# A fused attention and two-layer expert kernel: fewer and larger loads for attention, v on GpSimd's queue, and the stage's order planned anew

## The chip, the cores and the metric

The kernel runs on one core of a Trainium2 chip. The metric is the device time of one execution in microseconds (us), the median of several runs. One execution is also profiled, and the trace of that one is read here.

## The reference, cut to what matters

Three parts follow each other. Attention runs over 4 batches of 12 heads (448 positions, head size 64) with a soft cap. A dense part multiplies two projections and folds w3 and w_out behind them. A routed part sends every token through one of 8 experts.

```python
scores = cap * np.tanh((q @ k.T / sqrt(64)) / cap)
attn = softmax(scores) @ v                      # 4 x 12 heads, 448 x 64
x = attn as (1792, 768)
x = ((x @ w1) * (x @ w2)) @ w3 @ w_out          # w1, w2: 768 x 1024; w3: 1024 x 1024; float64 inputs
e = argmax(x @ w_gate + modality_bias[modality_id])
out = gate * (relu(x @ m1[e]) @ m2[e])          # 8 experts
```

The weights w1, w2, w3 and w_out are float64 in memory. The kernel turns them into float32 with integer operations on VectorE.

## The kernel before, in words

The change lies in the first stage, which holds attention and, beside it, work on the weights that attention does not depend on.

Attention goes by pairs of heads, 24 of them. For pair p the kernel loads k, q and v (`load_k`, `load_q`, `load_v`, lines 431 to 448), turns k and q with TensorE (`tr_k` L461, `tr_q` L475) and copies the results out of PSUM (`k_out`, `q_out`). The scores come in four blocks of keys c = 3, 0, 1, 2 (`score`, L488). ScalarE takes tanh (L493, L496 for the short block 3) and exp (L499) of each block. TensorE multiplies the blocks with v (`pv`, L508), the last block of one pair together with the first scores of the next (`pv_score`). VectorE adds the blocks for the softmax sums (`psum`, L524 to L528), TensorE spreads them (`sum_mm`, L535), and the results are stored (`sum_store` L544, `pair_store` L555).

Beside it stand three chains. Fourteen chunks of w_out, w1 and w2 are loaded (`load1`, tile raw, L289), made float32 (`narrow_a` L224 on ScalarE or L226 on VectorE, `narrow_b` L234 to L244), split into a rounded part wh (L252 or L254) and a rest wl (L329, on GpSimd). Sixteen chunks of w3 go the same way (`load_w3` L608, tile w3raw), are turned by TensorE (L620) and multiplied with w_out (`fold`, L649 to L651; 32 halves of 12 matmuls). The eight chunks of w_out are also multiplied with w_gate (`tr_wo` L585, `wo_gate` L593).

The order on every engine is not written by hand. A planner, class `Schedule`, takes each piece of work as a task with an engine (or several to choose from), a cost in ns, a key, and the tasks and buffers that it waits for. It repeatedly takes the task that can start earliest by its own costs, among equals the one with the smallest key, and writes its instructions at the end of its engine's queue. Keys count quarter pairs: pair p stands at 4p. So a changed cost or key moves instructions on all engines. On the chip each engine then works through its queue strictly in that order.

Buffers bound how far the stage runs ahead: two score tiles in PSUM (sc), two pairs of raw k and q, three v tiles, two raw weight chunks, two w3 chunks. A load of the chunk after next waits until the chunk in its buffer is used up. All loads and stores of the stage are issued from SyncE's queue (SP). TensorE keeps running dummy turns (L751) until the first k arrives.

After the stage come the dense part (L1001 to L1035) and the routed part (L1165 to L1216), which the change leaves as they are.

Of the kernel before, what the change touches and what calls it, by code (L numbers as in the profile page):

```python
# [120 lines left out]
def attention_moe_moe_kernel(  # L121
# [608 lines left out]
    def leave_at2():  # L730
# [32 lines left out]
    cap_in = add("SP", 475, -7 + 0.6, load_cap, dma=5)
    wg_in = add("SP", 475, -4, load_wg, dma=100)
    cap_in = add("DVE", 144, -100, inverse, [cap_in])


# [12 lines left out]
            wo_u[c] = ws.part  # L780
    for c in range(NW):
        u = c // 2
        key = (3 + 5.0 * c) if c < 8 else (10 + 10.0 * c)
        raw, y, un = ("wraw", c), ("y", c), ("unit", u)
        t = add("SP", 475, key - 2, ws.load1, take=[raw], use=[raw], dma=2185, deps=[ld])
        ld = t
        t = add({'ACT': (830, 0), 'DVE': (600, 300)}, 0, key, ws.abs1, [t] + ([ca] if c else []), take=[y], use=[raw, y])
        ca = t
        t = add({'DVE': (630, 0)}, 0, key, lambda eng: ws.narrow1(0, ENG[eng]), [t] + cn3[-1:], use=[raw, y])
        for i in range(1, 4):  # L790
            t = add("DVE", 630 if i == 1 else 950, key, do(narrow_c, c, i), [t], use=[raw, y])
        cn3.append(t)
        if c < 8:
            tt, tp = [("tr", "o", c, j) for j in range(2)], ("tr", "g", c)
            kg = key + 3.0
            cps = []
            for j in range(2):
                x = add("PE", 320, kg, do(tr_wo, c, j), [cn3[-1], *gate[-1:], *cps[-1:]], take=[tt[j], *([] if j else [("th", "o", c)])], use=[tt[j], y, ("th", "o", c)])
                cps.append(add({'ACT': (500, 0), 'DVE': (520, 300)}, 0, kg, lambda eng, c=c, j=j: wo_copy(c, j, eng), [x], use=[tt[j], ("th", "o", c)]))
# [22 lines left out]
    for p in range(NP + 1):  # L822
# [4 lines left out]
            dep, take, use = [ex[3], lv], [pk], [pk, ("th3", p - 1), ("v", p - 1)]  # L827
        if p < NP:
            k0, kk = 4 * p - 7, 4 * p - 4.0
            lk = add("SP", 1900, k0, do(load_k, p), take=[raw], use=[raw], dma=640)  # L830
            lq = add("SP", 950, k0 + 0.1, do(load_q, p), [(lk, 0)], use=[raw], dma=640)
            lv = add("SP", 1900, k0 + 4.0, do(load_v, p), [(lk, 0)], take=[vk], use=[vk], dma=640)
            t = add("PE", 380, 4 * p - 4.2, do(tr_k, p), [lk], take=[hk], use=[hk, raw])
            kl = add({'DVE': (620, 0), 'ACT': (530, 300)}, 0, kk, lambda eng, p=p: k_out(p, eng), [t], take=[kt], use=[hk, kt])
            t = add("PE", 380, 4 * p - 4.2, do(tr_q, p), [lq], take=[hq], use=[hq, raw])
            last_at2.append(t)
            ql = add({'DVE': (620, 0), 'ACT': (530, 300)}, 0, kk, lambda eng, p=p: q_out(p, eng), [t], take=[qt], use=[hq, qt])
            dep, take, use = dep + [kl, ql], take + [("sc", p, 3)], use + [("sc", p, 3), kt, qt]
        joint = add("PE", 770, 4 * p, do(pv_score, p), dep, take=take, use=use, mode="tiles")
        if p:  # L840

            for c in range(3):
                vl[p - 1, c] = add("PE", 770, 4 * p + c + 0.8, do(pv, p - 1, c), [ex[c], joint, vl.get((p - 1, c - 1))],
                                   use=[pk, ("th", p - 1, c), ("v", p - 1)], mode="tiles")
            smk = ("sc", "s", p - 1)
            sm = add("PE", 770, 4 * p + 2.9, do(sum_mm, p - 1), [ad], take=[smk], use=[smk, ("sums", p - 1)], mode="tiles")
            t = add({'ACT': (950, 0), 'DVE': (1000, 0)}, 0, 4 * p - 1, lambda eng, p=p: sum_out(p - 1, eng), [sm], take=[("smt", p - 1)], use=[smk, ("smt", p - 1)])
            ss = add("SP", 950, 4 * p, do(sum_store, p - 1), [t], use=[("smt", p - 1)], dma=25)
            t = add("ACT", 530, 4 * p - 2, do(pv_copy, p - 1), [vl[p - 1, 2]], take=[("pvs", p - 1)], use=[pk, ("pvs", p - 1)])
            po[p - 1] = add("DVE", 620, 4 * p - 2, do(pv_out, p - 1), [t], use=[pk, ("pvs", p - 1)])  # L850
            st[p - 1] = add("SP", 475, 4 * p, do(pair_store, p - 1), [po[p - 1]], use=[("pvs", p - 1)], dma=640)
            last_at1 += [sm, ss] if p > NP - 2 else []
            b, r = divmod(p - 1, H // 2)
            if r == H // 2 - 1 and b < B - 1:
                t = add("SP", 475, 4 * p, lambda b=b: rs_t.__setitem__(b, sums_in(b)), [ss], dma=100)
                t = add("DVE", 500, 4 * p, lambda b=b: sums_add(rs_t[b]), [t])
                last_at2.append(add("SP", 475, 4 * p, lambda b=b: sums_out(b, rs_t[b]), [t], dma=100))
        if p == NP:
            break
        ex, ad = {}, None  # L860
# [6 lines left out]
            t = add("ACT", 600 if c == 3 else 950, i + 0.2, do(p_tanh, p, c), [t, cap_in], take=[th], use=[sc, th])  # L867
            ex[c] = add("ACT", 580 if c == 3 else 950, i + 1.1, do(p_exp, p, c), [t], use=[th])
        for c in (1, 2, 3):
            ad = add("DVE", 620 if c == 3 else 1080, 4 * p, do(psum, p, c), [ex[c], *([ex[0]] if c == 1 else []), ad],  # L870
                     take=[sk] if c == 1 else [], use=[sk, ("th3", p) if c == 3 else ("th", p, c), *([("th", p, 0)] if c == 1 else [])])


# [17 lines left out]


    fs, wl_, fe = {}, {}, {}
    FK = lambda n, half: 4 * (4 + 0.62 * (2 * n + half)) + 2.3
    prev = None
    for n, (f, g) in enumerate(SWEEP):
        key = 12 + n * 5.5
        raw, r_, h_, w_ = ("w3raw", n), ("w3r", n), ("tr", "w", n), ("w3t", n)
        t = add("SP", 475, key - 3, do(load_w3, n), take=[raw], use=[raw], dma=1456)
        t = add({'ACT': (660, 0), 'DVE': (610, 300)}, 0, key, lambda eng, n=n: abs_w3(n, eng), [t], take=[r_], use=[raw, r_])  # L900
# [421 lines left out]
```

## Time and profile before

| what | us |
|---|---|
| median of three runs (986.35, 988.36, 1000.87) | 988.36 |
| the profiled execution | 979.18 |
| its span, first to last instruction | 977.5 |

The span stands for the kernel from its first to its last instruction; 1.68 us of the profiled execution lie around it. The first stage ends at about 323.5 us of the span, where the dense part's matmuls begin. In the rows an engine is PE (TensorE; PEld its weight loads), DVE (VectorE), ACT (ScalarE), POOL (GpSimd) or SP (SyncE). A q behind the name is the engine's sequencer, which issues DMAs. PEclk is TensorE's granted clock as a share of full speed. What stands behind "<-" is the event that ended an engine's idle time.

### The profile page before, as it was taken

Reading aid. Unit: us, or ns where it says so; the run is one execution under the profiler, and the core shown is the slowest. Engines: PE = TensorE matmul, PEld = TensorE weight load, DVE = VectorE, ACT = ScalarE, POOL = GpSimd, SP = SyncE. Lnnn points to the kernel's source line nnn. Section 1 sums busy time; section 2 is a strip of 40 time slices with the busy share of each in tenths; the row PEclk is TensorE's granted clock in tenths of the full one; section 3 lists DMA queues with packets and bytes.
Section 4 is the critical chain, followed back from the end, with each engine's and each line's share of the span. In section 5 each row is a group of like instructions: output and inputs, shape, how many; then the busy total and the mean of one; then the engine's idle time right before and its main releaser. Section 6 shows DMA issues by size and latency. Waiting matters only on the chain. (4 is left out here: it accounts for less than half of the span.)

```text
span 977.5 us, 13972 instructions
## 1 busy us (share of the span) xinstructions
PE 925.5 (95%) x5618; PEld 758.1 (78%) x5618; DVE 467.1 (48%) x668; ACT 377.0 (39%) x447; POOL 189.1 (19%) x114
## 2 busy tenths in 40 slices
PE   7789998999989899999999999999989999999994
PEld 4336665556544799999999999999879899889893
DVE  3678988695666477732005422110652533423410
ACT  4777777686857232222222211111421422322400
POOL 0111100020000112122542351300622311302011
PEclk9999999999999999999999999999999999999998
DMA  4755867665645556535633241301662491682411
GB/s 118 228 167 162 234 191 209 188 184 137 178 143 168 142 162 193 146 114 179 171 99 118 67 128 33 113 38 44 165 157 57 160 178 43 196 146 60 150 24 39
DMA packets 131736, 132.73 MB, mean 136 GB/s; under 512 B 61988, under 2 KB 114616, under 8 KB 131669
## 3 DMA queue, kind: packets, MB, share of 16 engines
q1 hardware_dynamic: 122388, 120.10, 42.9%
q0 software_dynamic: 9280, 11.71, 5.5%
q8 instruction: 46, 0.75, 0.3%
q14 instruction: 22, 0.17, 0.1%
HBM read 102.13 MB, written 30.19 MB: 135 GB/s over the span
## 5 line engine op out<-in xcount | busy, mean ns | idle before, releaser
L1002 PE MATMUL acc<-xT,wh 128*128 128x448 f32 x384 | 141.7, 369 | 0.7 <-DVE xT L936 0.7
L1001 PE MATMUL acc<-xT,wh 128*128 128x448 f32 x384 | 140.5, 366 | 1.9 <-ACT xT L934 1.9
L1003 PE MATMUL acc<-xT,wl 128*128 128x448 f32 x384 | 141.5, 368 | 0.0
L329 DVE TENSOR_TENSOR wl<-raw,wh 128x1536 fp32r<-128x1536 f32 (+1 forms) x42 | 73.5, 1758 | 121.3 <-ACT wh L252 121.3
L252 ACT CAST wh<-raw 128x1536 fp32r<-128x1536 f32 (+1 forms) x48 | 70.3, 1480 | 115.0 <-DMA raw<-in_moe_w_dram 82.6
L488 PE MATMUL sc<-QT,KT 64*64 64x448 f32 x672 | 93.2, 563 | 12.3 <-ACT th L493 5.9
L1208 PE MATMUL acc<-wl,hT 128*124 128x384 f32 x256 | 86.5, 338 | 3.7 <-DVE wl L329 3.7
L499 ACT ACTIVATE th<-th,capb 128x448 f32<-128x448 f32 (+1 forms) x96 | 89.3, 955 | 0.9
L508 PE MATMUL pv<-th,vt 64*64 64x448 f32 x672 | 89.0, 558 | 0.0
L1207 PE MATMUL acc<-wh,hT 128*124 128x384 f32 x256 | 87.6, 342 | 0.0
L1209 PE MATMUL acc<-wh,hT 128*124 128x384 f32 x256 | 86.5, 338 | 1.0 <-DVE hT L1186 1.0
L493 ACT ACTIVATE th<-sc,icap 128x896 f32<-128x896 f32 x72 | 71.5, 1007 | 23.5 <-PE sc L488 23.3
L1001 PEld LDWEIGHTS acc<-xT,wh 128*128 128x128 f32 x384 | 72.4, 189 | 9.2 <-ACT xT L934 2.6
L1002 PEld LDWEIGHTS acc<-xT,wh 128*128 128x128 f32 x384 | 72.6, 189 | 7.6 <-DVE xT L936 1.1
L1003 PEld LDWEIGHTS acc<-xT,wl 128*128 128x128 f32 x384 | 72.6, 189 | 5.5
L1033 PE MATMUL acc<-wh,gT 128*128 128x388 f32 x224 | 76.4, 341 | 0.0
L1034 PE MATMUL acc<-wl,gT 128*128 128x388 f32 x224 | 76.0, 339 | 0.0
L1035 PE MATMUL acc<-wh,gT 128*128 128x388 f32 x224 | 76.0, 339 | 0.0
L1181 PE MATMUL acc<-xsT,wh 128*128 128x496 f32 x192 | 74.7, 389 | 0.0
L1183 PE MATMUL acc<-xsT,wl 128*128 128x496 f32 x192 | 74.6, 389 | 0.0
L1182 PE MATMUL acc<-xsT,wh 128*128 128x496 f32 x192 | 74.4, 388 | 0.0
L1011 POOL TENSOR_TENSOR gT<-a,gT 128x896 fp32r<-128x896 f32 x16 | 43.8, 2739 | 145.7 <-DVE gT L1010 145.7
(159 smaller groups left out, 1543.2 us busy)
## 6 DMA issues: line engine op xcount, KB each, us to landing
raw<-in_moe_w_dram SPq DMA_DIRECT2D x48, 768.0 KB
w3raw<-in_moe_w_dram SPq DMA_DIRECT2D x16, 512.0 KB
raw<-w_scr SPq DMA_DIRECT2D x8, 776.0 KB
raw<-in_moe_w_out_dram SPq DMA_DIRECT2D x8, 768.0 KB
w_scr<-y SPq DMA_DIRECT2D x16, 384.0 KB
raw<-w_scr SPq DMA_DIRECT2D x8, 768.0 KB
q<-in_q_dram SPq DMA_DIRECT2D x48, 112.0 KB
x_scr<-pvs SPq DMA_DIRECT2D x24, 224.0 KB
```

Of the source, the lines that this page charges most:

```text
L488: mm(sc[rows_of(side(p, j, g)), g, :S], lhsT=KT[p][rows_of(j), o:o + D], rhs=QT[p][rows_of(j), :], start=True, stop=True)
L499: nc.scalar.activation(tht[p, c], tht[p, c], ACTF.Exp, scale=capb)
L508: mm(pvb[p][rows_of(j), r, :S], lhsT=vt[p][rows_of(r), NC * g + c, :], rhs=tht[p, c][rows_of(r), g, :] if c < NB else tht[p, c][rows_of(r) ...
L1001: mm(acc[:, ft, :S], lhsT=wh[:, o:o + P], rhs=x[:, 0, d, :], start=(d == 0), stop=False)
L1002: mm(acc[:, ft, :S], lhsT=wh[:, o:o + P], rhs=x[:, 1, d, :], start=False, stop=False)
L1003: mm(acc[:, ft, :S], lhsT=wl[:, o:o + P], rhs=x[:, 0, d, :], start=False, stop=(d == KD - 1))
L1033: mm(acc[:, hf, :HA], lhsT=gt[:, 0, f, ts], rhs=wh[:, o:o + HA], start=(f == 0), stop=False)
L1034: mm(acc[:, hf, :HA], lhsT=gt[:, 0, f, ts], rhs=wl[:, o:o + HA], start=False, stop=False)
L1035: mm(acc[:, hf, :HA], lhsT=gt[:, 1, f, ts], rhs=wh[:, o:o + HA], start=False, stop=(f == KF - 1))
L1207: mm(acc[:TP, hf, :HT], lhsT=ht[:, 0, f, cs], rhs=wh[:, o:o + HT], start=(f == 0), stop=False)
L1208: mm(acc[:TP, hf, :HT], lhsT=ht[:, 0, f, cs], rhs=wl[:, o:o + HT], start=False, stop=False)
L1209: mm(acc[:TP, hf, :HT], lhsT=ht[:, 1, f, cs], rhs=wh[:, o:o + HT], start=False, stop=(f == KF - 1))
```

## The change

In `load_k` the loads of the two heads are joined: one DMA for each half of the keys, so two in place of four for each pair. In `load_q` one DMA loads both heads in place of two, and that of pair 0 is issued from ScalarE's queue. The four DMAs of `load_v` are issued from GpSimd's queue. The bytes are the same, and so are the tiles that they land in.

The planner's numbers are changed to go with that, and others beside them: a DMA issue costs 630 instead of 475, the chunks of w_out get keys that lie 4.0 apart in place of 5.0, the turns of k and q are due a quarter pair earlier, the products with v 1.6 quarter pairs later, w3 and the folds are shifted, ScalarE is preferred less for the first step on w_out's chunks, and more for their copies.

```diff
         for g in range(2):
-            for j in range(2):
-                nc.sync.dma_start(k2[rows_of(g), 0:NC - g, j, :], keys(heads(k, p), g)[j])
+            nc.sync.dma_start(k2[rows_of(g), 0:NC - g], keys(heads(k, p), g).rearrange("h p c d -> p c h d"))
...
     def load_q(p):
-        for j in range(2):
-            nc.sync.dma_start(raw_qkv[p][1][:, :, j, :], heads(q, p)[j].rearrange("(p c) d -> p c d", c=NC))
+        eng = nc.sync if p else nc.scalar
+        eng.dma_start(raw_qkv[p][1], heads(q, p).rearrange("h (p c) d -> p c h d", c=NC))
...
             for j in range(2):
-                nc.sync.dma_start(vt[p][rows_of(side(p, j, g)), NC * g:NC + NB * g, :], keys(heads(v, p), g)[j])
+                nc.gpsimd.dma_start(vt[p][rows_of(side(p, j, g)), NC * g:NC + NB * g, :], keys(heads(v, p), g)[j])
...
-        key = (3 + 5.0 * c) if c < 8 else (10 + 10.0 * c)
+        key = (4.0 * c + 3) if c < 8 else (10 + 10.0 * c)
...
-            lv = add("SP", 1900, k0 + 4.0, do(load_v, p), [(lk, 0)], take=[vk], use=[vk], dma=640)
+            lv = add("POOL", 2800, k0 + 4.0, do(load_v, p), [(lk, 0)], take=[vk], use=[vk], dma=640)
```

Three places show how instructions move. The first is SyncE's queue from the first chunk of w_out (raw) to the second; k_180, q_181 and their like are the raw tiles of one pair, vt is v. Before:

```order
L289 DMA raw<-in_moe_w_out_dram 128x1536
L438 DMA k_180<-in_k_dram 64x4x64 x2
L438 DMA k_180<-in_k_dram 64x3x64 x2
L448 DMA vt<-in_v_dram 64x256 x2
L448 DMA vt<-in_v_dram 64x192 x2
L442 DMA q_181<-in_q_dram 112x4x64 x2
L438 DMA k_238<-in_k_dram 64x4x64 x2
L438 DMA k_238<-in_k_dram 64x3x64 x2
L448 DMA vt<-in_v_dram 64x256 x2
L448 DMA vt<-in_v_dram 64x192 x2
L442 DMA q_239<-in_q_dram 112x4x64 x2
L289 DMA raw<-in_moe_w_out_dram 128x1536
```

The same stretch of SyncE's queue after the change:

```order
L289 DMA raw<-in_moe_w_out_dram 128x1536
L607 DMA w3raw<-in_moe_w_dram 128x1024 x2
L437 DMA k_180<-in_k_dram 64x8x64
L437 DMA k_180<-in_k_dram 64x6x64
L441 DMA q_181<-in_q_dram 112x8x64
L437 DMA k_202<-in_k_dram 64x8x64
L437 DMA k_202<-in_k_dram 64x6x64
L441 DMA q_203<-in_q_dram 112x8x64
L289 DMA raw<-in_moe_w_out_dram 128x1536
```

Between the two chunks 20 DMAs stood, and now 8 stand, two of them the first w3 chunks, which stood behind the second w_out chunk before.

The second place is TensorE's queue from the start of the kernel: the dummy turns, the turns of k and q of pairs 0 and 1, the first scores (sc). Before:

```order
L751 MATMUL tr<-ident 128x128 x18
L461 MATMUL tr<-ident,k_99 128x128 x3
L461 MATMUL tr<-ident,k_99 128x64
L751 MATMUL tr<-ident 128x128 x12
L475 MATMUL tr<-ident,q_100 128x112 x4
L461 MATMUL tr<-ident,k_127 128x128 x3
L461 MATMUL tr<-ident,k_127 128x64
L488 MATMUL sc<-QT,KT 64x448 x10
L475 MATMUL tr<-ident,q_128 128x112 x4
L488 MATMUL sc<-QT,KT 64x448 x6
```

TensorE's queue from the start after the change:

```order
L750 MATMUL tr<-ident 128x128 x14
L460 MATMUL tr<-ident,k_99 128x128 x3
L460 MATMUL tr<-ident,k_99 128x64
L750 MATMUL tr<-ident 128x128 x16
L474 MATMUL tr<-ident,q_100 128x112 x4
L460 MATMUL tr<-ident,k_122 128x128 x3
L460 MATMUL tr<-ident,k_122 128x64
L474 MATMUL tr<-ident,q_123 128x112 x4
L487 MATMUL sc<-QT,KT 64x448 x16
```

The turn of pair 1's q now stands ahead of the first scores, where it stood between two groups of them.

The third place is GpSimd's queue at the last chunks of w1 and w2, where L329 makes the rest wl of one chunk. Before:

```order
L329 TENSOR_TENSOR wl<-y_1260,wh 128x6x128
L329 TENSOR_TENSOR wl<-y_1467,wh 128x6x128
L329 TENSOR_TENSOR wl<-y_1590,wh 128x6x128
L329 TENSOR_TENSOR wl<-y_1695,wh 128x6x128
L329 TENSOR_TENSOR wl<-y_1754,wh 128x6x128
L329 TENSOR_TENSOR wl<-y_2125,wh 128x6x128
```

GpSimd's queue at the last four of these chunks after the change:

```order
L329 TENSOR_TENSOR wl<-y_1303,wh 128x6x128
L447 DMA vt<-in_v_dram 64x256 x2
L447 DMA vt<-in_v_dram 64x192 x2
L329 TENSOR_TENSOR wl<-y_1392,wh 128x6x128
L329 TENSOR_TENSOR wl<-y_1569,wh 128x6x128
L329 TENSOR_TENSOR wl<-y_2110,wh 128x6x128
L447 DMA vt<-in_v_dram 64x256 x2
L447 DMA vt<-in_v_dram 64x192 x2
```

The loads of v now stand between the subtractions, so a load can be held up by a subtraction that waits for its chunk, and the other way round.

## Rows read from the trace of the kernel before

**Rows 1.** Windows: the stage's first 80 us, its rest, the parts behind it.
```profile
core 0: us, PE busy (x) PEld busy (x) DVE busy (x) ACT busy (x) POOL busy (x), PEclk, DMA share, GB/s
0.00:80.00 80.00, 62.59 (x491) 30.94 (x491) 50.66 (x82) 52.66 (x69) 7.89 (x10) 0.94 0.60 167
80.00:323.50 243.50, 230.80 (x1863) 138.87 (x1859) 183.65 (x287) 172.83 (x226) 21.39 (x21) 0.99 0.62 177
323.50:977.50 654.00, 632.13 (x3272) 588.27 (x3268) 232.79 (x301) 151.55 (x153) 159.78 (x83) 0.99 0.43 117
```

**Rows 2.** What ended TensorE's idle times from 0 to 82 us: total, times, longest.
```profile
PE sc L488 <- ACT th L493: 5.9, 3, 2.8
PE tr L475 <- DMA q<-in_q_dram: 4.1, 2, 2.2
PE tr L461 <- DMA k<-in_k_dram: 3.8, 3, 2.4
```

**Rows 3.** Timeline of SyncE's DMA issues, 0 to 14 us: start, duration, what.
```profile
0.86 2.63 SPq L438 DMA_DIRECT2D k<-in_k_dram  x4
3.54 1.30 SPq L442 DMA_DIRECT2D q<-in_q_dram  x2
...
6.01 2.51 SPq L438 DMA_DIRECT2D k<-in_k_dram  x4
...
11.13 1.26 SPq L442 DMA_DIRECT2D q<-in_q_dram  x2
```

**Rows 4.** Timeline of TensorE, 0 to 30 us: start, duration, idle before in brackets.
```profile
10.24 0.72 PE L461 MATMUL tr<-ident,k 128*128 128x128 f32 x4 [2.37 <-DMA k<-in_k_dram]
10.89 2.69 PE L488 MATMUL sc<-QT,KT 64*64 64x448 f32 x20
15.83 0.98 PE L475 MATMUL tr<-ident,q 112*128 112x112 f32 x4 [2.25 <-DMA q<-in_q_dram]
```

**Rows 5.** What ended ScalarE's idle times from 30 to 82 us.
```profile
ACT w3r L224 <- DMA w3raw<-in_moe_w_dram: 6.3, 2, 3.5
...
ACT y L224 <- DMA raw<-in_moe_w_out_dram: 2.4, 2, 1.5
```

**Rows 6.** Timeline of SyncE's DMA issues, 42 to 60 us.
```profile
43.79 2.77 SPq L448 DMA_DIRECT2D vt<-in_v_dram  x4
46.61 2.60 SPq L438 DMA_DIRECT2D k<-in_k_dram  x4
...
52.57 0.54 SPq L608 DMA_DIRECT2D w3raw<-in_moe_w_dram  x1
```

**Rows 7.** Timeline of ScalarE, 50 to 60 us.
```profile
56.88 0.66 ACT L224 ACTIVATE w3r<-w3raw 128x512 f32<-128x512 f32 x1 [3.45 <-DMA w3raw<-in_moe_w_dram]
57.45 0.99 ACT L493 ACTIVATE th<-sc,icap 128x896 f32<-128x896 f32 x1
```

**Rows 8.** Timeline of TensorE, 53 to 60 us.
```profile
58.49 0.98 PE L488 MATMUL sc<-QT,KT 64*64 64x448 f32 x8 [2.79 <-ACT th L493]
```

**Rows 9.** Windows of 20 us within the stage, columns as in the first group.
```profile
40.00:60.00 20.00, 14.36 (x117) 6.37 (x110) 13.60 (x25) 14.46 (x21) 2.16 (x2) 0.91 0.60 175
60.00:80.00 20.00, 19.12 (x158) 8.42 (x158) 19.37 (x28) 17.18 (x23) 3.40 (x2) 0.92 0.59 174
```

**Rows 10.** Timeline of ScalarE, 0 to 20 us.
```profile
8.31 1.28 ACT L496 ACT_TABLE_LOAD   x1 [8.31 <-DVE icap L759]
```

**Rows 11.** Groups of GpSimd's instructions, whole span: count, busy us, mean ns, idle before.
```profile
L1152 POOL DMA_INDIRECT xsr<-x_scr,idx x16 | 28.6, 1787 | 17.5 <-DMA idx<-tab_scr 10.9 <-issue 3.6 <-ACT a L1006 3.0
L329 POOL TENSOR_TENSOR wl<-y,wh 128x768 fp32r<-128x768 f32 x14 | 27.9, 1996 | 192.1 <-ACT wh L252 150.2 <-DVE wh L254 40.2 <-issue 1.8
...
L1149 POOL DMA_DIRECT2D idx<-tab_scr x4 | 2.4, 594 | 19.9 <-DMA out_dram<-y,idx 10.0 <-issue 9.9
```

**Rows 12.** Timeline of GpSimd, 55 to 64 us.
```profile
59.67 1.86 POOL L329 TENSOR_TENSOR wl<-y,wh 128x768 fp32r<-128x768 f32 x1 [15.00 <-ACT wh L252]
```

**Rows 13.** Timeline of VectorE, 57 to 64 us.
```profile
59.76 2.18 DVE L234 TENSOR_SCALAR y<-y 128x768 f32<-128x768 f32 x1
```

More of the change, by code (lines that the diff above doesn't have):

```diff
@@ L761, in inverse @@
         )
[L763 to L764 removed]
+    cap_in = add("SP", 630, -7 + 0.6, load_cap, dma=5)
+    wg_in = add("SP", 630, -4, load_wg, dma=100)
     cap_in = add("DVE", 144, -100, inverse, [cap_in])
@@ L782, in attention_moe_moe_kernel @@
         u = c // 2
-        key = (3 + 5.0 * c) if c < 8 else (10 + 10.0 * c)
+        key = (4.0 * c + 3) if c < 8 else (10 + 10.0 * c)
         raw, y, un = ("wraw", c), ("y", c), ("unit", u)
-        t = add("SP", 475, key - 2, ws.load1, take=[raw], use=[raw], dma=2185, deps=[ld])
+        t = add("SP", 630, key - 2, ws.load1, take=[raw], use=[raw], dma=2185, deps=[ld])
         ld = t
-        t = add({'ACT': (830, 0), 'DVE': (600, 300)}, 0, key, ws.abs1, [t] + ([ca] if c else []), take=[y], use=[raw, y])
+        t = add({'ACT': (920, 600), 'DVE': (600, 0)}, 0, key, ws.abs1, [t] + ([ca] if c else []), take=[y], use=[raw, y])
         ca = t
@@ L829, in attention_moe_moe_kernel @@
             k0, kk = 4 * p - 7, 4 * p - 4.0
-            lk = add("SP", 1900, k0, do(load_k, p), take=[raw], use=[raw], dma=640)
-            lq = add("SP", 950, k0 + 0.1, do(load_q, p), [(lk, 0)], use=[raw], dma=640)
-            lv = add("SP", 1900, k0 + 4.0, do(load_v, p), [(lk, 0)], take=[vk], use=[vk], dma=640)
-            t = add("PE", 380, 4 * p - 4.2, do(tr_k, p), [lk], take=[hk], use=[hk, raw])
+            lk = add("SP", 1260, k0, do(load_k, p), take=[raw], use=[raw], dma=640)
+            lq = add("SP" if p else "ACT", 630, k0 + 0.1, do(load_q, p), [(lk, 0)] if p else [], use=[raw], dma=640)
+            lv = add("POOL", 2800, k0 + 4.0, do(load_v, p), [(lk, 0)], take=[vk], use=[vk], dma=640)
+            t = add("PE", 380, 4 * p - 5.2, do(tr_k, p), [lk], take=[hk], use=[hk, raw])
             kl = add({'DVE': (620, 0), 'ACT': (530, 300)}, 0, kk, lambda eng, p=p: k_out(p, eng), [t], take=[kt], use=[hk, kt])
-            t = add("PE", 380, 4 * p - 4.2, do(tr_q, p), [lq], take=[hq], use=[hq, raw])
+            t = add("PE", 380, 4 * p - 5.2, do(tr_q, p), [lq], take=[hq], use=[hq, raw])
             last_at2.append(t)
@@ L869, in attention_moe_moe_kernel @@
         for c in (1, 2, 3):
-            ad = add("DVE", 620 if c == 3 else 1080, 4 * p, do(psum, p, c), [ex[c], *([ex[0]] if c == 1 else []), ad],
+            ad = add("DVE", 660 if c == 3 else 1120, 4 * p + 0, do(psum, p, c), [ex[c], *([ex[0]] if c == 1 else []), ad],
                      take=[sk] if c == 1 else [], use=[sk, ("th3", p) if c == 3 else ("th", p, c), *([("th", p, 0)] if c == 1 else [])])
@@ L893, in attention_moe_moe_kernel @@
     fs, wl_, fe = {}, {}, {}
-    FK = lambda n, half: 4 * (4 + 0.62 * (2 * n + half)) + 2.3
+    FK = lambda n, half: 18 + 2.48 * (2 * n + half) + 2.3
     prev = None
     for n, (f, g) in enumerate(SWEEP):
-        key = 12 + n * 5.5
+        key = 5.4 * (n + 2) + 3
         raw, r_, h_, w_ = ("w3raw", n), ("w3r", n), ("tr", "w", n), ("w3t", n)
-        t = add("SP", 475, key - 3, do(load_w3, n), take=[raw], use=[raw], dma=1456)
-        t = add({'ACT': (660, 0), 'DVE': (610, 300)}, 0, key, lambda eng, n=n: abs_w3(n, eng), [t], take=[r_], use=[raw, r_])
+        t = add("SP", 630, key - 3, do(load_w3, n), take=[raw], use=[raw], dma=1456)
+        t = add({'ACT': (660, -300), 'DVE': (610, 0)}, 0, key, lambda eng, n=n: abs_w3(n, eng), [t], take=[r_], use=[raw, r_])
         t = add({'DVE': (500, 0)}, 0, key, lambda eng, n=n: conv_w3(n, 0, eng), [t], use=[raw, r_])
@@ L906, in attention_moe_moe_kernel @@
         wl_[n] = t = add("DVE", 600, key - 4, do(w3_l, n), [t], use=[h_, w_])
-        lp = add("SP", 475 if g else 0, key - 3, do(part, n), [fs[n - KF]] if g else [], take=[("wst", n)], use=[("wst", n)],
+        lp = add("SP", 630 if g else 0, key - 3, do(part, n), [fs[n - KF]] if g else [], take=[("wst", n)], use=[("wst", n)],
                  lag=0, dma=1092 if g else None)
@@ L910, in attention_moe_moe_kernel @@
             fo = ("sc", "f", n)
-            late = vl[NP - 2, 2] if n == FN - 1 and half else None
+            late = vl[NP - 2, 2] if n == FN - 1 else None
             prev = add("PE", 2130, FK(n, half), do(fold, n, half), [t, units[2 * g], units[2 * g + 1], *augs[4 * g:4 * g + 4], prev, late],
@@ L914, in attention_moe_moe_kernel @@
             fe[n, half] = add("DVE", 560, 0, do(fold_out, n, half), [prev, lp], use=[fo, ("wst", n)])
-        fs[n] = add("SP", 475, key, do(fold_store, n), [fe[n, 0], fe[n, 1]], use=[("wst", n)], dma=1092)
+        fs[n] = add("SP", 630, key, do(fold_store, n), [fe[n, 0], fe[n, 1]], use=[("wst", n)], dma=1092)
     def leave_at1():
```

16 lines of the change are left out of this document (8 added, 8 removed).

## The prediction

> **What bounds the kernel now.** I read the windows first. The reader is to see in them that TensorE is busy nearly throughout, and that its free time is not spread evenly [rows 1]. Behind the first stage, from 323.5 us on, it works 632.13 of 654 us, and nothing there is touched. In the first stage it is idle for 80 − 62.59 = 17.4 us of the first 80 us, but only 243.5 − 230.8 = 12.7 us of the following 243.5 us. The granted clock adds to it: 0.94 of full speed over the first 80 us means 80 × 0.06 = 4.8 us of lost time, against 0.01 × 243.5 = 2.4 us later. So the first quarter of the stage loses 17.4 + 4.8 = 22.2 us and the other three quarters together 15.1 us. The place to look is the first 80 us.
>
> Second, the waits of TensorE in that stretch [rows 2]. Two kinds carry it: turns that wait for the DMAs of q and k (4.1 + 3.8 = 7.9 us) and scores that wait for ScalarE's tanh to free one of the two score tiles (5.9 us).
>
> Third, SyncE's own timeline. In the first 12 us it issues DMA after DMA without a pause, about 0.63 us each (2.51 us for 4) [rows 3]. Pair 1's k is fully issued at 8.52 us and TensorE gets it at 10.24; pair 1's q is issued by 12.39 us and used at 15.83 [rows 3, 4]. So a load lands 1.7 to 3.4 us behind its issue, and TensorE's 2.37 and 2.25 us of waiting are time that these loads stood in the queue. Around 50 us the same queue delays ScalarE. From 43.79 us SyncE is busy with v, with k and with what stands behind them, and the third w3 chunk is issued only at 52.57 [rows 6]. ScalarE, which works in order, waits 3.45 us for that chunk at a step that TensorE doesn't need soon, and the tanh behind it starts at 57.45 [rows 7]. TensorE's next scores wait 2.79 us for exactly that tanh [rows 8]. In this stretch ScalarE waits 6.3 + 2.4 = 8.7 us for raw weights [rows 5]. Both kinds of wait thus lead to one cause, SyncE's issue time, and after such gaps the granted clock is low: 0.91 and 0.92 from 40 to 80 us [rows 9].
>
> **The change part by part.**
>
> *Joined loads and v moved.* A pair costs SyncE 4 issues for k, 2 for q, 4 for v, 2 for sums and 1 for the result: 13 × 0.63 = 8.2 us, and a weight chunk or two on top. After the change it is 2 + 1 + 0 + 2 + 1 = 6, or 3.8 us. A joined load moves twice the bytes in runs of the same length. No row shows its issue; by the nearest row it takes 0.63 us, since the issue of a larger tile (a w3 chunk) takes 0.54 [rows 6]; that I take. The upper end is 1.3 (as two), at which k and q would save nothing and only v's 2.5 us a pair would be gone; the lower end, 0.54, saves half a microsecond more a pair. For the DMA engines the sum of bytes is unchanged; their share of 0.60 in the first 80 us would rise to about 0.70 if the same work fitted in 69 us, and the later window holds 0.62 with TensorE 95% busy [rows 1]. I cost that at nothing; if it is not hidden it appears as late weights.
>
> *Pair 0's q from ScalarE.* One issue of 0.63 us at a time when ScalarE has nothing to do (the first scores come at 10.89 [rows 4]). It costs nothing and takes 1.3 us of SyncE's queue from ahead of the cap and pair 1.
>
> *The head.* SyncE now issues k (2), cap, w_gate, k (2), q: 0.86 + 7 × 0.63 = 5.3 us. Pair 1's q lands 1.7 to 3.4 us later, at 7.0 to 8.7, and its turn stands ahead of the first scores. I put these at 8.4 us against 10.89, and the first tanh at 9.0. What is late next is ScalarE.
>
> *The first 80 us as a whole.* ScalarE does 52.66 us of work there, 1.3 of it a table load [rows 10] which the new order puts ahead of the first scores with a copy of k. The remaining 51.4 us must fit behind 9.0. In its densest 20 us ScalarE worked 17.18, or 86% [rows 9], in a window where loads were no longer late. At 86% the 51.4 us take 59.8, so the work of the first 80 us ends at 68.8: 11.2 us gained. Bounds: at 80%, 9.0 + 64.3 = 73.3 and 6.7 us gained; at 95%, 9.0 + 54.1 = 63.1 and 16.9 us gained. I take 86% because that row is the nearest. TensorE's own work there, 62.59 − 4.8 = 57.8 us, would fit as well. VectorE's 50.66 us fit behind 9.0 at its own densest 97% (19.37 of 20) by 61 us, so it isn't the last.
>
> *v on GpSimd's queue.* GpSimd gets 96 DMA issues. The nearest row is its plain DMA of 594 ns; its indirect one takes 1787 [rows 11]. So 57 us, at most 172 us, are added to 27.9 us of subtractions in a stage of 312 us. It is hidden in GpSimd's idle time at either end. A new wait arises where a load stands behind a subtraction that waits for its chunk. Behind it stand further loads and subtractions, and TensorE's product with v waits for the load. Three v tiles mean that a load can be issued once the pair three before is done, over a pair ahead of its use, some 13 us (323.5 / 24). I cost it at nothing, from −1 (v no longer queues behind weights) to +6 us. GpSimd can also hold up VectorE: a narrowing step took 2.18 us beside a subtraction of 1.86 that had begun just before [rows 12, 13]. If each of the some 24 v issues of the first 80 us did so for its 0.594, VectorE would have 14 us more, 50.66 + 14 = 65, ending at 9.0 + 65 / 0.97 = 76 us, and 4 us of gain would be left. That is the upper end. I take none, since the row shows it for a subtraction that reads and writes full tiles, which a DMA issue does not.
>
> The Trainium skill, SBUF — State Buffer, section "SBUF: two separate sides", warns of the other direction: while VectorE runs an operation in its two-port mode, GpSimd can't write the descriptors of its DMAs, and the section "A bandwidth-pool intuition that's wrong" gives such a DMA about 3.1 us in place of 0.62. By that figure, as an estimate, 96 issues would take 298 us and fill GpSimd, which is rival C below; no row of before shows a GpSimd DMA beside such an operation, though the rows on the subtraction agree that the two engines exclude each other.
>
> *The new order behind 80 us.* The same matmuls, the same tasks, other places. Idle 12.7 and clock 2.4 us could become anything from 9 to 21 us. I take no change, −6 to +6.
>
> Sum: −11.2 + 0 + 0. The profiled execution would take 979.18 − 11.2 = 968 us. Its median stands 9.2 us higher at 988.36, so the forecast for the median is 977 us.
>
> The Trainium skill, DMA: Bandwidth & Descriptors, section "Issuing engines are not separate DMA queues", says that issuing from several engines saves only the sequencer's time, usually small beside the DMA itself. The rows agree on what is saved and differ on its size: here that time was the last wait in most of 7.9 + 5.9 = 13.8 of the first 80 us. By the rule's "small" the sum would be near 0.
>
> **The rivals.**
>
> *A. The gain is larger.* ScalarE runs at 95% and the new order also saves the 6 us behind 80 us: 16.9 + 6 = 23, giving 965. For it: the late weights were 8.7 us of what ScalarE waited [rows 5]. Against: it has never been that dense over 20 us.
>
> *B. The gain is hidden.* VectorE, which turns w_out's chunks that now come faster, stays at the 68% of 40 to 60 us (13.60 of 20 [rows 9]): 9.0 + 50.66 / 0.68 = 83.5 us, no gain in the stretch; with the clock back, some 2 us: 986. For it: 19.37 of 20 in the next window shows that VectorE is nearly full once weights arrive. Against: that same density.
>
> *C. Slower: v's loads fill GpSimd.* If each issue takes so long that GpSimd's queue is the last, the stage lasts 27.9 + 96 × t. It decides from t = (312 − 27.9) / 96 = 2.96 us; at 3.3 us the stage takes 345 instead of 323.5, and the kernel 1010. Place: TensorE's products with v, which wait for their loads from the middle of the stage on. For it: that the two engines exclude each other [rows 12, 13]. Against: 0.594 and 1.787 are what such issues took, with VectorE in use too.
>
> **How the numbers follow.** Forecast 0.61 (its own range 971 to 984, from 16.9 us of gain to 4), A 0.17, B 0.17, C 0.05. Two per cent of 988.36 are 19.8 us, about what a measurement of this kernel can tell from no change; that is a bound at 968.6 and 1008. Faster holds nearly all of A: 0.17. Slower holds C and little else: 0.05. The rest is 0.78. The range takes in half of A and B whole: 964 to 989.
>
> **What would show it.** Right: TensorE's waits for q and k in the first 80 us fall from 7.9 to under 3 us, ScalarE's waits for raw weights from 8.7 to under 4 us, the first scores start near 8.4 us, the dense part begins near 312 us, and the windows behind 80 us lose about 15 us as before. Wrong: TensorE's waits keep their sum under other names (VectorE's sums, copies or narrowing), GpSimd's DMA issues take well over 1.8 us, or the dense part begins near 312 us but the end does not move.

## The result, and the profile after

The changed kernel takes 971.17 us (median of 4 runs, 968.68 to 977.17) against 987.36 for before (4 runs on the same chip, 979.43 to 1000.87). The ratio is 0.985, with a 95% interval of 0.981 to 0.990. That is 16.2 us between the medians, where 11.2 were forecast; 977 us was predicted in a range of 964 to 989. One of before's four runs, 1000.87, is a slow one; without it before's median is 986.35 and the difference 15.2 us.

The two profiled executions hide most of this. Their spans are 977.5 and 975.5 us, only 2.0 us apart. The profiled execution of after is the slowest of its four runs, at a mean granted clock of 0.975 (the other three had 0.983 to 0.987), and that of before, 979.18 us, is faster than all of its four, at 0.986. At one clock for both, 0.011 × 975.5 = 10.7 us more would lie between them, which brings the 2.0 to 12.7; this is an estimate, since it lets the whole span follow the clock. So the traces are read here for where the time went within them, and the medians for how much.

Windows of after: the first 80 us, the rest of the stage, what lies behind it (columns as in rows 1).

```profile
0.00:80.00 80.00, 70.81 (x512) 41.75 (x516) 58.02 (x91) 55.95 (x77) 28.09 (x40) 0.87 0.76 190
80.00:320.35 240.35, 226.58 (x1842) 136.74 (x1834) 178.89 (x279) 169.50 (x220) 52.46 (x87) 0.99 0.61 173
320.35:975.50 655.15, 634.19 (x3268) 590.86 (x3268) 231.97 (x300) 150.20 (x151) 159.77 (x83) 0.98 0.42 116
```

The first row answers to the first of [rows 1]. TensorE's idle time falls from 17.4 to 9.2 us, 8.2 won, and VectorE and ScalarE do 7.4 and 3.3 us more work in the same 80 us. The granted clock falls from 0.94 to 0.87: 10.4 us lost to it, where 4.8 were lost before. In this execution the clock takes back 5.6 of the 8.2 us. Behind 80 us TensorE stands idle for 13.8 us until the dense part, which begins at 320.35; in the trace of before it begins at 325.39 and that idle time is 14.6. So the stage is 5.0 us shorter (the forecast had its end near 312), and the 655.15 us behind it are 3.0 longer than before, at a clock of 0.98 instead of 0.99.

What ended TensorE's idle times in after, 0 to 82 us (total, times, longest), and then ScalarE's from 30 to 82 us:

```profile
PE tr L460 <- DMA k<-in_k_dram: 2.4, 2, 2.0
PE tr L592 <- DVE KT L254: 1.7, 1, 1.7
...
PE tr L619 <- DVE wl L598: 1.3, 1, 1.3
...
PE sc L487 <- ACT th L492: 0.6, 1, 0.6
...
PE tr L474 <- DMA q<-in_q_dram: 0.4, 1, 0.4
```

```profile
ACT woT L252 <- PE tr L584: 4.7, 3, 2.2
ACT smt L252 <- PE sc L534: 2.9, 2, 2.6
ACT th L492 <- PE sc L487: 2.2, 3, 1.1
ACT w3r L224 <- PE tr L619: 1.3, 1, 1.3
```

The waits for k and q were 7.9 us [rows 2] and are 2.8; the scores' wait for tanh was 5.9 and is 0.6. ScalarE's 8.7 us behind late raw weights [rows 5] are gone: TensorE and not a DMA is what it now waits for, 11.1 us by these four lines. Part of that is the new order and not the loads. It gives the first step on more of w_out's chunks to VectorE, and the kernel with the order only, below, shows the waits for raw weights there.

The head went another way than forecast. SyncE's DMA issues in after, 0 to 14 us, and TensorE's timeline, 0 to 16 us:

```profile
0.87 1.68 SPq L437 DMA_DIRECT2D k<-in_k_dram  x2
...
3.73 1.29 SPq L437 DMA_DIRECT2D k<-in_k_dram  x2
5.07 0.70 SPq L441 DMA_DIRECT2D q<-in_q_dram  x1
```

```profile
1.53 3.22 PE L750 MATMUL tr<-ident 128*128 128x128 f32 x14 [1.53 <-DVE ident L217]
6.77 0.72 PE L460 MATMUL tr<-ident,k 128*128 128x128 f32 x4 [2.02 <-DMA k<-in_k_dram]
7.42 3.16 PE L750 MATMUL tr<-ident 128*128 128x128 f32 x16
10.38 0.95 PE L474 MATMUL tr<-ident,q 112*128 112x112 f32 x4
...
12.58 2.69 PE L487 MATMUL sc<-QT,KT 64*64 64x448 f32 x20
```

Pair 1's q is issued by 5.77 us, near the forecast of 5.3. But k of pair 0, fully issued at 2.55, is turned only at 6.77, 4.2 us behind its issue. The 16 dummy turns behind it then take 3.16 us, behind the gap of 2.02. The granted clock of these microseconds, by windows:

```profile
7.00:9.00 2.00, 2.00 (x14) 1.76 (x13) 0.85 (x3) 0.00 (x0) 1.23 (x3) 0.75 1.25 200
9.00:11.00 2.00, 2.00 (x12) 2.00 (x11) 0.00 (x0) 0.00 (x0) 0.31 (x1) 0.50 1.17 256
```

It was 0.75 and then 0.50. The first scores come at 12.58, in before at 10.89 [rows 4].

### The profile page after: what moved, and what is told of

Read it like the earlier page. It is cut to its first block, busy times and chain, and to the rows that moved or that the text cites. A ratio compares the mean times of both kernels' runs of the same rounds, so it can differ in the third digit from the quotient of the medians.

```text
span 975.5 us, 13895 instructions
## 1 busy us (share of the span) xinstructions
PE 931.6 (95%) x5618; PEld 769.3 (79%) x5618; DVE 468.9 (48%) x668; ACT 375.6 (39%) x447; POOL 240.3 (25%) x210
## 5 line engine op out<-in xcount | busy, mean ns | idle before, releaser
L329 DVE TENSOR_TENSOR wl<-raw,wh 128x1536 fp32r<-128x1536 f32 (+1 forms) x42 | 73.5, 1758 | 113.3 <-ACT wh L252 113.3
L447 POOL DMA_DIRECT2D vt<-in_v_dram x96 | 50.7, 542 | 151.5 <-PE pv L507 149.9
L1180 PE MATMUL acc<-xsT,wh 128*128 128x496 f32 x192 | 74.7, 389 | 0.0
```

## The experiments

The theory that I took into them (theory 1): SyncE's issue time, 0.63 us for each DMA, is what the first quarter of the stage waits for, and the change wins by issuing less there. Its rivals: the new order of the engines wins it; the place of v wins it; or what a DMA moves, and how, counts and not its issue. Each group of runs was timed against before on its own chip, so before has a median for each group: 986.13, 986.95 and 985.97 us. Where two groups are compared below, that difference of up to 1 us comes on top of the noise.

**The parts apart.** Four kernels: the three load functions of the change in the old order; the new order with the old load functions; the change with v back on SyncE; the change with k and q in halves again.

```diff
 # loads only: before, with load_k, load_q, load_v of the change
 # order only: the change, with load_k, load_q, load_v of before
 # v on SyncE: the change, and in load_v
-                nc.gpsimd.dma_start(vt[p][...
+                nc.sync.dma_start(vt[p][...
 # k and q in halves: the change, and in load_k (load_q likewise, pair 0 on SyncE too)
-            nc.sync.dma_start(k2[rows_of(g), 0:NC - g], keys(heads(k, p), g).rearrange("h p c d -> p c h d"))
+            for j in range(2):
+                nc.sync.dma_start(k2[rows_of(g), 0:NC - g, j, :], keys(heads(k, p), g)[j])
```

> The kernel before with only the three load functions of the change: k in two DMAs and q in one for each pair, the first q from ScalarE's queue, v from GpSimd's. The planner still sees the old tasks, so TensorE, VectorE and ScalarE keep the order of the kernel before. Theory 1 (SyncE's issue time was what the first 80 us waited for): most of the gain is here, 8 to 13 us faster than before; TensorE's waits for k and q and ScalarE's waits for raw weights in the first 80 us fall from 7.9 and 8.7 us to under 4 each. Rival (the new order brings the gain): within 3 us of before, with the same waits under other names.

> The changed kernel with the three load functions of the kernel before: 4 + 2 + 4 DMAs for each pair, all from SyncE's queue, in the new order of tasks. Theory 1: the gain is gone or turned into a loss, 0 to 15 us slower than before, since the new order asks SyncE for weights earlier still; waits of TensorE for k and q of 8 us or more in the first 80 us. Rival (the order brings the gain): 8 us or more faster than before.

> The changed kernel with v's four DMAs for each pair issued from SyncE's queue again; k and q stay joined. SyncE then issues 10 DMAs for a pair in place of 6 (13 before). If issue time counts issue by issue, about half of the gain stays: 5 to 9 us faster than before. Rival (moving v off SyncE is what counts, since it waits there for TensorE to free a v tile and holds up the loads behind it): no more than 3 us of gain stay. Second rival (GpSimd's early v loads take the DMA engines from the first k and q): as fast as the change or faster, with the first scores ahead of 12.6 us.

> The changed kernel with k and q loaded by 4 + 2 DMAs from SyncE's queue again, the first q too; v stays on GpSimd's queue. SyncE issues 9 DMAs for a pair in place of 6. If issue time counts issue by issue, about half of the gain stays: 6 to 10 us faster than before, and the head of the kernel is later than in the change by some 2 us. If v on SyncE's queue was the whole of it: as fast as the change within 3 us.

| kernel | issues per pair on SyncE | us, median | ratio to before, 95% |
|---|---|---|---|
| before | 13 | 986.13 | |
| loads only, old order | 6 | 971.70 | 0.984 [0.980, 0.989] |
| order only | 13 | 985.95 | 1.000 [0.998, 1.003] |
| change, v on SyncE | 10 | 970.25 | 0.984 [0.980, 0.988] |
| change, k and q in halves | 9 | 979.56 | 0.994 [0.991, 0.997] |

The loads alone give the whole gain and the new order alone gives none: the order is out as a cause. With v back on SyncE nothing is lost, so v's loads standing in that queue are not what counted either. One sign that I had named failed: with the loads only, ScalarE still waits 6.3 us for raw weights (8.7 before, expected under 4), and the kernel gains 14.4 us all the same. But the last two rows are no straight line in the number of issues. Ten with k and q joined give all of it, nine with v moved and k and q in halves give 40%. So I asked next whether that is the issues at all.

**One load change at a time in the old order, and v held back.**

```diff
 # k and q joined, v on SyncE: before, with load_k and load_q of the change
 # v moved only: before, and in load_v
-                nc.sync.dma_start(vt[p][...
+                nc.gpsimd.dma_start(vt[p][...
 # v held: loads only, and in load_v ahead of the DMAs
+        if p < 3:
+            held = at1.tile([1, 1], F32, name="held", tag="held", bufs=1)
+            nc.gpsimd.tensor_copy(held, raw_qkv[p][1][0:1, 0, 0, 0:1])
```

> Before, with k by two DMAs and q by one; v stays on SyncE and the order of the other engines is the old one: 10 issues for a pair. Theory 1 (SyncE's issue time, any issue counts alike): 3 of 7 issues saved, so 40% of the gain, about 980 us. Theory 2 (what counts is how soon the last k and q of the first pairs have landed, so joining them is the whole of it): about 971 us, ratio 0.985, TensorE's waits for k and q in the first 82 us under 4 us.

> Before, with v issued by GpSimd and nothing else changed: 9 issues for a pair on SyncE. Theory 1: 4 of 7 issues saved, about 978 us. Theory 2: k and q still stand in 6 issues a pair, and v's loads now compete with them at the head: at most a third of the gain, 981 to 987 us, waits for k and q still over 4 us.

> The three load functions of the change in the old order (as in the run with the loads only), and GpSimd issues v of pairs 0 to 2 only once that pair's q has landed (a 1x1 copy on GpSimd reads q first). If v's early loads crowd the first k and q: the first k turn near 5.3 us instead of 6 to 7, the first scores some 1 us sooner, 968 to 971 us. If they don't: as the loads alone, 971.7 us within 2; if v is then late, TensorE waits for v tiles and it is slower than 973.

Measured against 986.95 for before: joined only 971.88, ratio 0.987 [0.984, 0.990]; v moved only 974.19, 0.990 [0.986, 0.994]; loads with v held 969.63, 0.986 [0.982, 0.989]. Either half of the change thus gives nearly everything by itself, and both together (971.70) no more than one. Both theories missed: theory 1 in its linear form expected 980 and 978, theory 2 expected at least 981 for v alone. In the old order it looks like a threshold. Added up from its timeline, SyncE's issuing takes 66.8 of the first 80 us before, 61.6 with k and q joined, 52.7 with v moved and 35.6 with both; the first step buys nearly everything. But that share alone doesn't decide: the change with k and q in halves issues for only 50.1 us and gains 6.6. What ends last beyond the first step? Windows from 20 to 60 us, of the loads only, of the loads with v held, and of k and q joined only:

```profile
20.00:60.00 40.00, 36.92 (x329) 18.51 (x322) 39.66 (x58) 38.08 (x53) 16.00 (x20) 1.00 0.80 209
```

```profile
20.00:60.00 40.00, 36.52 (x338) 17.56 (x333) 38.45 (x62) 36.93 (x51) 16.96 (x20) 1.00 0.89 228
```

```profile
20.00:60.00 40.00, 35.59 (x282) 16.36 (x278) 30.77 (x49) 32.60 (x45) 5.50 (x3) 0.87 0.71 197
```

In the first two VectorE works 39.66 and 38.45 of 40 us, ScalarE 38.08 and 36.93: they are full, and more could not be won there. With k and q joined only they are not, 30.77 and 32.60, and yet that kernel is as fast by its median. So why issues saved beyond the first step buy nothing is not shown.

Holding v back set the first k turn at 6.13 instead of 7.16 us and the first scores at 9.41 instead of 11.97 in the profiles, and is worth 2 us at most by the medians, within their uncertainty. The same edit was made in the changed kernel itself:

> The changed kernel, with v of pairs 0 to 2 issued by GpSimd only once that pair's q has landed (a 1x1 copy on GpSimd reads q first); the order of the other engines is the change's. If early v loads crowd the first k and q: the first k turn near 5.3 us instead of 6.77, the first scores near 11 us instead of 12.58, 966 to 970 us. If they don't: 971 us, the first scores near 12.6.

It took 972.66 us, 0.986 [0.981, 0.990]: no difference from the change. In its profile, the longest of its six runs (982.46), the first k turn came at 6.42 us instead of 6.77 and the first scores at 12.03 instead of 12.58. So v's early loads are a small part of the late head there (in the old order 1.0 us of the first k turn), and the 5.3 us that I expected for k was wrong.

**SyncE's issue time given back almost without bytes.** To the loads only (the old order) come seven blank DMAs for a pair, of 4 KB that nobody reads, so SyncE issues 13 again, while k, q and v travel as in the change.

```diff
+    def blank(p):
+        t = nc.dram_tensor(f"blank{len(blanks)}", (16, D), F32).ap()
+        blanks.append(t)
+        nc.sync.dma_start(t, q[0, 0, 0:16])      # or nc.gpsimd
...
             nc.sync.dma_start(k2[rows_of(g), 0:NC - g], ...)
+            blank(p)
...
         eng.dma_start(raw_qkv[p][1], ...)
+        blank(p)
...
+        for _ in range(4):
+            blank(p)
```

> The three load functions of the change in the old order, and on SyncE seven blank DMAs of 4 KB for a pair, between DRAM tensors that nobody reads, at the places where before had its other halves of k and q and its v: SyncE issues 13 for a pair again, but the bytes of k, q and v come as in the change. Theory 1 (issue time): the gain is gone, 984 to 988 us, and TensorE's waits for k and q are back at 6 us or more. Theory 2 in the form that the joined load itself lands sooner: most of the gain stays, 971 to 975 us.

> The run with seven blank DMAs for a pair, but GpSimd issues them: same 168 transfers of 4 KB, other sequencer. If it is SyncE's issue time that costs (theory 1): the 27 us of loss are gone, 970 to 976 us (a little of it may come back where GpSimd's subtractions or v get late). If the transfers themselves cost (write receipts, ring space, DMA engines): 990 us or more.

> Blank DMAs on SyncE for pairs 0 to 7 only, whose k is loaded in about the first 80 us: 56 of 168. If the cost of SyncE's issues sits in the first quarter of the stage, as the prediction has it: nearly the whole loss, 990 to 998 us. If it is spread evenly: a third of 27 us, 979 to 982 us.

> Blank DMAs on SyncE for pairs 8 to 23 only: 112 of 168. If the cost sits in the first quarter: 970 to 977 us. If it is spread evenly: two thirds of 27 us, 987 to 991 us.

| blank DMAs | us, median | ratio to before, 95% |
|---|---|---|
| 168 on SyncE, all pairs | 998.59 | 1.013 [1.009, 1.017] |
| 168 on GpSimd, all pairs | 971.82 | 0.986 [0.982, 0.991] |
| 56 on SyncE, pairs 0 to 7 | 987.32 | 1.002 [1.000, 1.005] |
| 112 on SyncE, pairs 8 to 23 | 976.47 | 0.992 [0.988, 0.995] |

The first row stands against 986.95 for before, the others against 985.97. The same 168 transfers cost 26.9 us from SyncE (998.59 − 971.70) and nothing measurable from GpSimd, so it is SyncE's queue and not the transfers. Nor do the blanks make a load in that queue land later: k is turned 3.8, 3.3 and 3.5 us behind its issue for pairs 0 to 2, and 4.6 for pair 0 with the loads only. That leaves the time of issuing. A third of the blanks, in the first pairs, takes back the whole gain (987.32 − 971.70 = 15.6 us; 0.28 us an issue). The other two thirds cost 4.8 us alone (0.04 an issue), about the uncertainty of the two medians, but 11.3 on top of the first third (998.59 − 987.32).

The place can be read more directly. TensorE's queue holds the same order in before and in these kernels, so one can ask when the 491 matmuls of before's first 80 us [rows 1] are done. Windows up to that moment, with the loads only, with the blanks in pairs 8 to 23, and with those in pairs 0 to 7:

```profile
0.00:67.40 67.40, 59.38 (x491) 31.43 (x491) 52.63 (x82) 50.96 (x69) 26.84 (x42) 1.00 0.83 200
0.00:68.30 68.30, 60.90 (x491) 31.29 (x491) 52.89 (x82) 51.29 (x69) 26.12 (x42) 0.95 0.80 197
0.00:85.00 85.00, 68.88 (x491) 34.36 (x491) 51.71 (x82) 52.84 (x70) 23.56 (x39) 0.86 0.60 160
```

The work of before's first 80 us takes 67.4 us with the loads only, 68.3 with blanks behind pair 7 and 85.0 with blanks up to pair 7; VectorE has done 82 instructions each time, as in before. Medians and traces agree: the gain is won in the first quarter of the stage, and issues of SyncE there take it back.

SyncE's queue, 5 to 20 us, then what ended TensorE's and ScalarE's idle times, 0 to 82 us, with all blanks on SyncE:

```profile
5.68 0.65 SPq L444 DMA_DIRECT2D k<-in_k_dram  x1
6.37 0.64 SPq L435 DMA_DIRECT2D blank<-in_q_dram  x1
...
7.74 3.16 SPq L435 DMA_DIRECT2D blank<-in_q_dram  x5
10.95 0.65 SPq L449 DMA_DIRECT2D q<-in_q_dram  x1
```

```profile
PE sc L498 <- ACT th L503: 7.6, 2, 7.2
PE tr L471 <- DMA k<-in_k_dram: 4.8, 4, 1.8
PE tr L485 <- DMA q<-in_q_dram: 1.9, 1, 1.9
```

```profile
ACT w3r L224 <- DMA w3raw<-in_moe_w_dram: 10.1, 2, 8.2
```

A blank DMA holds the queue for 0.63 us (3.16 for 5), as long as a joined k (0.65). And the pattern of before is back: TensorE waits for tanh, and ScalarE stands before a late w3 chunk, as in [rows 2, 5].

With the blanks on GpSimd, the first 80 us and GpSimd's group of blanks from the page (count, busy us, mean ns, idle before):

```profile
0.00:80.00 80.00, 71.06 (x561) 38.77 (x562) 62.00 (x95) 59.78 (x80) 59.33 (x104) 0.96 0.79 194
...
L435 POOL DMA_DIRECT2D blank<-in_q_dram x168 | 85.7, 517 | 21.1 <-DMA blank<-in_q_dram 9.1
```

GpSimd is busy for 59.33 of 80 us, and VectorE still does 62.00 us of work.

One number sorts all kernels here: how long TensorE waits for k and q in the first 82 us of the profile. It is 0.6 to 3.8 us in the nine with a median up to 976.5, 4.3 in the change with k and q in halves (979.56), and 5.7 to 7.9 in the four from 985.95 up, before among them. This is one profile each, and a wait that goes with the time is not yet its cause.

Three things stay open. All blanks on SyncE end 11.6 us behind before, with as many issues, where I expected 984 to 988; the surplus lies behind the first pairs, since the blanks in pairs 0 to 7 alone end level with before (expected: 990 to 998). The two kernels with v moved and k and q in halves stand at 0.990 (old order) and 0.994 (new order); whether the new order suffers more from halved loads, because pair 1's q turn stands ahead of the first scores there, was not tried. And no kernel here beats the change by more than the measurement's uncertainty: 969.63 and 970.25 are the nearest.

## Why the prediction was right or wrong

**What bounds the kernel: right as to place and queue; the way over ScalarE is not shown.** That the time lies in the first quarter of the stage and is SyncE's issuing is what the blank DMAs show: 15.6 us for pairs 0 to 7, 4.8 for the rest, nothing from GpSimd. I had two ways by which it reaches TensorE: loads of k and q, and late weights that hold up ScalarE and so a tanh. The first goes with the time in every kernel. The second doesn't. Waits for raw weights from 0 to 82 us, with the order only, and then with k and q joined only:

```profile
ACT w3r L224 <- DMA w3raw<-in_moe_w_dram: 0.7, 1, 0.7
DVE y L226 <- DMA raw<-in_moe_w_out_dram: 9.9, 3, 4.5
```

```profile
ACT y L224 <- DMA raw<-in_moe_w_out_dram: 5.6, 2, 3.8
ACT w3r L224 <- DMA w3raw<-in_moe_w_dram: 2.2, 2, 1.7
DVE y L226 <- DMA raw<-in_moe_w_out_dram: 4.3, 3, 2.5
```

The order takes this wait off ScalarE, and the kernel is no faster (985.95); with k and q joined only the two engines wait 12.1 us for weights, and it is as fast as the change. Whether late weights cost anything by themselves stays open.

**An issue of a joined load, 0.63 us: right.** Pair 0's two took 1.68, pair 1's two 1.29, a joined q 0.65 to 0.70, so issue time doesn't follow the bytes.

**The landing of a joined load: wrong, and not costed.** I let it land 1.7 to 3.4 us behind its issue, as the loads of before did. TensorE got pair 1's k 1.7 us behind its last issue in before [rows 3, 4]. With joined loads every k that TensorE waited for in the first 24 us came later than that. The turns of k that waited for their DMA, in the kernel with k and q joined only (no v from GpSimd there):

```profile
6.58 0.72 PE L460 MATMUL tr<-ident,k 128*128 128x128 f32 x4 [1.19 <-DMA k<-in_k_dram]
...
16.37 0.72 PE L460 MATMUL tr<-ident,k 128*128 128x128 f32 x4 [1.33 <-DMA k<-in_k_dram]
```

The first was fully issued at 2.55 us and the second at 10.50: 4.0 and 5.9 us to the turn. In the run with v back on SyncE it was 3.4 and 6.9, with the blanks 3.8, 3.3 and 3.5 for pairs 0 to 2, in after 4.2 and, for pair 2, 9.7. The joining is not all of it, since halves came later too where more was moving: 1.8 us twice with the order only, but 2.4 and 2.8 with v moved only, and 3.2 and 6.2 in the change with k and q in halves. The DMA share of the first 20 us, a count of the view that can pass 1, is 0.50 in before and 0.49 with the order only, 0.59 with the blanks, 0.84 with the halves in the new order and 1.02 in after. Joining and fuller DMA engines were not taken apart.

**The head, first scores at 8.4 us: wrong, 12.58.** The step that failed is the sum from the issue of pair 1's q alone. k of pair 0 came 1.4 us later than in before (6.77 against 5.34), the new order has 16 dummy turns behind it, and at the lowered clock these took 3.16 us; only then follow the turns that the sum began with. The first tanh came at 13.60 us instead of 9.0. The medians show no price for it beyond their uncertainty: the change and the kernel with v held, with its first scores at 9.41, differ by 1.5 us.

**The first 80 us, −11.2 us: right in kind and size; of its two terms one held.** 11.2 us lies inside the interval of the first comparison (10.2 to 19.3 us of 987), and the medians lean to more: 16.2 us there, and 14.4, 15.9 and 15.1 in the kernels with the loads only, with v back on SyncE and with k and q joined only. The trace of after redoes the sum. Windows to the moment at which ScalarE has done the 52.66 us of [rows 1], from the start and from its first tanh:

```profile
0.00:72.00 72.00, 62.81 (x469) 34.61 (x470) 54.73 (x86) 52.69 (x73) 26.27 (x39) 0.89 0.81 200
13.60:72.00 58.40, 52.85 (x415) 26.19 (x412) 52.13 (x78) 50.88 (x71) 19.24 (x21) 0.89 0.78 202
```

ScalarE works 50.88 of 58.40 us, 87%: the density of 86% held. The start was 4.6 us too early, and so 8.0 us are gained there in place of 11.2. The density is no constant: counted in the same way it is 92% with the loads only and 81% with k and q joined only. That the medians still show more than the trace is not this sum's doing. The profiled execution of before is some 7 us faster than before's medians and that of after 6.0 slower than its own, and that 977 came within 6 us of 971.17 is in part luck.

**The clock: not costed.** I took none of the clock's 4.8 us as won or lost in the forecast's sum. In the profile 5.6 us more are lost to it in the first 80 us; over the runs the clock went the other way: its median is 0.984 in the four runs of after, and 0.980 in the 23 of before beside the first experiments. Windows of after around two gaps of TensorE, of 1.72 us at 26.5 and of 1.28 at 68.9:

```profile
28.00:35.00 7.00, 6.74 (x36) 4.32 (x40) 6.22 (x12) 4.37 (x6) 0.00 (x0) 0.53 0.70 195
...
70.00:76.00 6.00, 5.80 (x21) 5.74 (x22) 3.52 (x6) 2.61 (x4) 1.82 (x1) 0.50 0.47 117
```

TensorE is busy for 6.74 of 7 and 5.80 of 6 us there, at about half its clock, the lower of its two levels (1.2 GHz); up to the gaps, from 24.00 to 26.50 and from 62.00 to 68.90, the clock is 1.00. In the profile of the loads with v held the clock is 1.00 over all of the first 80 us, though TensorE is idle for 6.97 us, once for 1.81 at a stretch; that execution took 961.01, the fastest of any. So a gap of 1 to 2 us can be followed by 6 to 7 us at about half the clock, and need not be; what decides is not shown here.

**v on GpSimd's queue, 0: right, and not needed.** GpSimd's DMA issues in after, from the page:

```profile
L447 POOL DMA_DIRECT2D vt<-in_v_dram x96 | 50.7, 542 | 151.5 <-PE pv L507 149.9
```

An issue takes 542 ns (594 in [rows 11]). GpSimd waits 149.9 us for free v tiles, and TensorE waits 0.2 us in all for its loads. Rival C, from 2.96 us an issue, is out: the longest of the 96 took 0.80 us. The 3.1 us that the Trainium skill gives for such a DMA (SBUF — State Buffer, section "A bandwidth-pool intuition that's wrong") is not seen in these issues. From issue to landing the 96 took 2.0 to 7.4 us, 3.1 in the median, and what part VectorE has in that the trace does not tell. Nor did the issues hold up VectorE, the prediction's upper end. Four issues of v in after, and a narrowing step of VectorE that falls among them:

```profile
25.07 2.13 POOL L447 DMA_DIRECT2D vt<-in_v_dram  x4
```

```profile
27.04 0.56 DVE L234 TENSOR_SCALAR y<-y 128x768 f32<-128x768 f32 x1
```

It took 0.56 us, where the same step beside a subtraction took 2.18 [rows 13], and the issues 0.53 each. Eight such steps (L226, L234) fall among issues of v in the stage: six took 0.41 to 0.56 us, and the two of 2.43 and 2.34 ran beside a subtraction as well.

**The new order, 0 ± 6: right.** Alone it is worth 1.000 [0.998, 1.003], and the change equals the loads in the old order (971.17 and 971.70). It also has a new stall of its own. ScalarE and TensorE in after, around 147 us:

```profile
147.25 0.89 ACT L224 ACTIVATE y<-raw 128x768 f32<-128x768 f32 x1 [4.77 <-DMA raw<-in_moe_w_dram]
...
148.97 0.89 ACT L252 COPY smt<-sc 128x896 f32<-128x896 f32 x1
```

```profile
149.92 1.01 PE L487 MATMUL sc<-QT,KT 64*64 64x448 f32 x2 [4.32 <-ACT smt L252]
```

ScalarE waits 4.77 us for a raw chunk that SyncE issued at 137.30, and TensorE 4.32 us for the copy queued behind. From 132.57 to 137.25 SyncE was issuing other DMAs, and the chunk then took 9.5 us to land, at a DMA share of 1.00 (137.00 to 147.20). It has the form of the stall in the first quarter, but issue time is only part of it.

**From the profile to the median, +9.2 us: wrong in its use.** I added the distance of before's profile from its median to the forecast. The profile of after (977.17) lies 6.0 above its own median. One execution's distance from the median is not the kernel's.

**The rivals.** B (no gain, since VectorE stays at 68%) is out: in after it works 19.10 of the 20 us from 40 to 60, 95%. A (965, ScalarE at 95% and 6 us behind 80 us) is out for after, with 87% and a median of 971.17. The rule on issuing engines (the Trainium skill, DMA: Bandwidth & Descriptors, section "Issuing engines are not separate DMA queues"), that issuing elsewhere saves only the sequencer's usually small time, was weighed against the rows and set aside as to size. The runs show both sides: from 13 issues a pair to 10 or 9 that time is worth 13 to 16 us (6.6 in the one kernel left open above), from 10 to 6 nothing.

## What to carry to other kernels

Where one queue issues loads for two chains at a rate of 0.63 us each and is busy for most of a stretch (here 66.8 of 80 us), blank DMAs on it measure what an issue costs there, and the same blank DMAs on another queue tell issue time from transfer. Don't expect the gain to go by the number of issues: in the old order three of 13 were enough and seven gave no more. A wait that vanishes from a profile is not yet a gain: the order alone took ScalarE's waits away and won nothing. Judge by medians of several runs where the granted clock differs from run to run; two single profiles would have shown 2 us of 16.

## What had not been expected of the hardware

A joined load of twice the bytes has the same issue time (0.65 us), but where TensorE waited for it at the kernel's head its tile came 3.3 to 9.7 us behind the issue, where the halves of before needed 1.7. Fuller DMA engines have a part in that, as the halves' own 2.4 to 6.2 us in two other kernels show.

SyncE's issue itself can stand. SyncE's issues in after, 10 to 24 us, and the window of 10 to 20 us:

```profile
12.11 5.63 SPq L437 DMA_DIRECT2D k<-in_k_dram  x2
...
19.83 1.30 SPq L437 DMA_DIRECT2D k<-in_k_dram  x2
```

```profile
10.00:20.00 10.00, 8.71 (x63) 3.83 (x61) 5.88 (x10) 6.55 (x9) 0.00 (x0) 0.93 1.15 268
```

The same two issues took 5.63 us at one place and 1.30 at the next. The first pair fell into a stretch in which the DMA engines' busy share was 1.15 in the view's count; whether the full engines held the queue was not tried.

The time of one kernel differs from run to run and goes with the mean granted clock: 968.68 us at 0.987 and 977.17 at 0.975 in the changed kernel, 961.01 at 0.992 and 974.45 at 0.984 in the one with v held.
